# A hand-kept global order of 975 steps is replaced by a new one, with other transfer rates in its planner

## The chip, the cores and the metric

The kernel runs on one core of a Trainium2 chip. The core has five engines that run beside each other and meet at semaphores: TensorE (PE in the profile; PEld is its weight load), VectorE (DVE), ScalarE (ACT), GpSimd (POOL) and SyncE (SP). Here SP does nothing but issue DMAs; ACT issues a few too. The metric is device time in microseconds (us), the median of several runs; smaller is better.

## What is computed

Polynomial-sketch attention over 4 batches, 4 heads, 1088 positions and head dimension 32, followed by a feed-forward layer on the 4352 tokens (width 128, hidden width 2048) with a rational activation:

```python
def phi(x):                                   # 8 x 8 sketch features of each position
    a = einsum('rd,bhsd->bhsr', S1, x)
    b = einsum('rd,bhsd->bhsr', S2, x)
    return einsum('bhsi,bhsj->bhsij', a, b).reshape(..., 64)
q_p, k_p = phi(q), phi(k)
kv  = einsum('bhsf,bhsd->bhfd', k_p, v)
z   = sum(k_p, axis=2)
x   = einsum('bhsf,bhfd->bhsd', q_p, kv) / (einsum('bhsf,bhf->bhs', q_p, z) + 1e-6)
h   = x @ w_in                                # 4352 x 128 by 128 x 2048
P   = a[0] + a[1]*h + a[2]*h*h + a[3]*h*h*h
Q   = 1 + |b[0]|*|h| + |b[1]|*h*h
out = (P / (Q + 1e-6)) @ w_out                # 2048 x 128
```

Inputs and output are float32.

## The kernel before

The whole program is a list of 975 steps, each for one engine: a DMA issue, a group of matmuls, an ACT or DVE instruction. `step(...)` and `dma(...)` append to the list; nothing is issued while it is built. At the end `run` sorts the steps by a number from the table `PLACE` and issues them in that order. Each engine works through its own steps strictly in this order, so `PLACE` decides who queues behind whom, on SP's and ACT's DMA queues too. Waits between engines follow from the data and from the buffers: a step that takes a buffer of a kind with few slots (`Buf("kq")` has 3, `v_sb` 1, `h`, `att` and `out` in PSUM 2 each, `a_all`, `b_all`, `sk_sb` and `sk_d` 2 each, `t` 16) takes the slot that has been free the longest and waits until its last reader is done.

The numbers given to a step besides its function (rank, cost, `rate`, `slack`, `early`, `behind`) belong to the planner that once computed `PLACE`. In the program itself they issue nothing and wait for nothing; `behind` and `after` are only used to assert that one step's place precedes another's. `ON_ACT` lists the numbers of steps that could run on ACT or DVE and run on ACT. `FILLS` says ahead of which places how many products of zeros (line L321) are put on PE.

What the steps do, with the lines of the profile:

- *Loads.* S1 and S2 (`s_raw`), k of the first batch (on ACT's queue), a first piece of q (256 of its 1088 columns), v in two halves, the rest of q, `w_out` in two halves (into the buffer `ln`), `w_in` in two halves, k of the second batch, then v and q of the second batch, and so on. All other loads are on SP's queue (L268).
- *keys*, once a batch: DVE transposes k (L415, L417), PE makes sketches (L435), ACT copies one factor (L440, `b_sk`), DVE multiplies to features `k_p` (L443), PE accumulates features by v (L454), ACT copies the sum to `kvz` (L471).
- *queries*, in pieces of up to 384 positions: DVE transposes q (L496). The first 512 positions are done "direct": PE writes both sketches expanded (L518), ACT copies (L523, L526), DVE multiplies (L530, L533). All later pieces are "spread": PE makes the plain sketches (L546), ACT copies them (L551, `sk_sb`), two DMAs put them to DRAM (`sk_d`), three DMAs get them back repeated (`a_all`, `b_all`), DVE multiplies (L554). Then, for both: products with kvz (L586), guard, inverse and quotient on DVE (L595, L599, L602), a transpose on PE (L608), a copy to `xT` on ACT (L615).
- *w_out* is converted to bf16 in five scaled versions of two halves each: ten steps, on ACT (L391 scaled, L393 plain) or DVE (L395 scaled).
- *a* and *b* are spread to all partitions by a product with ones (L377) and two ACT copies (L380, L381).
- *units*, 29 of them, of up to 6 blocks of 512 tokens: hidden products (L688), ACT evacuates them to bf16 (L692), then the activation: DVE takes |h| (L703), w = |b0| + |b1| |h| on DVE (L708) or ACT (L710), a product (L713), ACT ln and exp (L716, L719), a product with r (L728), and, in three ways of dividing the work ("modes"), further products on DVE (L731, L734, L737, L746, L749), p = a2 + a3 h on DVE (L723) or ACT (L725), the addition of a1 on DVE (L741) or ACT (L743). PE gathers with w_out (L784), DVE turns the result (L796), SP stores it (L808).

Of the kernel before, what the change touches and what calls it, by code (L numbers as in the profile page):

```python
# [20 lines left out]
def kernel(  # L21
# [15 lines left out]
    B, H, S, D = q.shape  # L37
# [87 lines left out]
    def d_four(n, ptr):  # L125
# [14 lines left out]
    LOADS = 1.3  # L140
# [5 lines left out]
    GET_SLACK = 0.9  # L146
# [67 lines left out]
    )  # L214
    ON_ACT = (
        24, 26, 28, 29, 31, 32, 328, 351, 379, 454, 478, 502, 535, 612, 636, 669, 688, 693, 744, 878, 889,
        914, 932, 946, 951, 953, 960,
    )
    FILLS = {5: 15, 14: 4, 66: 5, 70: 1}
# [36 lines left out]
    def flat(x, b):  # L256
        return x[b].rearrange("h (g j) d -> (h g) (j d)", g=32)
# [605 lines left out]
```

## Time and profile before

| | |
|---|---|
| median of 3 runs | 266.75 us (266.74 to 267.11) |
| profiled execution | 267.34 us; its span, from first to last instruction, 265.5 us |
| busy: PE, DVE, ACT | 257.2, 252.7, 248.4 us |
| moved by DMA | 20.13 MB, mean 76 GB/s; 202 to 331 GB/s in the first 13 us |

A row of a timeline gives start in us from the start of the span, duration in us, engine, line, operation, output <- input, shapes, count (rows that stand close together are merged), and in square brackets how long the engine had been idle before and what the profile thinks ended that. SPq is SP's issuing of DMAs. A row of waits gives the engine and line that waited, what for, us in total, times, the longest. A row of groups gives the form, xcount, then busy us and mean ns of one, then idle us before. A row of the chain gives start, duration and what the chain was in.

### The profile page before, as it was taken

The numbers are of one execution on the slowest core, as the hardware profiler recorded it, in microseconds if no ns is written. First come the engines' busy times: TensorE is split into PE (matmuls) and PEld (weight loads), VectorE is DVE, ScalarE is ACT, GpSimd is POOL, SyncE is SP. The second block draws the span as 40 slices with busy tenths as digits, with TensorE's granted clock in tenths as the row PEclk, the third lists the DMA queues.
The fourth block names the chain that finished last, engine by engine and source line by source line (L and its number), as shares of the span: only waits on it lengthen the run. The fifth ranks groups of instructions, "written<-read, shape, count | busy, mean of one in ns | idle before, by whom it ended". The sixth has DMA issues, their size and how long they took to land.

```text
span 265.5 us, 4239 instructions
## 1 busy us (share of the span) xinstructions
PE 257.2 (97%) x1663; PEld 140.4 (53%) x1663; DVE 252.7 (95%) x293; ACT 248.4 (94%) x209; POOL 2.7 (1%) x25
## 2 busy tenths in 40 slices
PE   7999999999999999999999999999999999999994
PEld 5767645644544464344445555444444476565682
DVE  3989899999999999999999999999999999999994
ACT  2499999999999999999999999999999999999991
POOL 4000000000000000000000000000000000000000
PEclk9999999999999999999999999999999999999998
DMA  7948344620556503035001522200002002010032
GB/s 202 331 151 223 121 127 118 159 61 0 145 131 168 164 2 108 13 79 131 28 6 44 150 65 46 41 0 0 0 10 32 0 0 40 4 29 11 0 52 40
DMA packets 29063, 20.13 MB, mean 76 GB/s; under 512 B 19316, under 2 KB 24948, under 8 KB 29044
## 3 DMA queue, kind: packets, MB, share of 16 engines
q1 hardware_dynamic: 28352, 19.24, 28.8%
q10 hardware_dynamic: 692, 0.62, 0.8%
q8 instruction: 13, 0.21, 0.4%
q14 instruction: 6, 0.05, 0.1%
HBM read 16.65 MB, written 3.21 MB: 75 GB/s over the span
## 4 chain that ended last, share of the span: by engine, by line
PE 35%; ACT 29%; DVE 21%; issue 8%; DMA 4%; SPq 1%; DVEq 0%; ACTq 0%
PE h_ps L688 21%; ACT t L692 7%; ACT ln L716 7%; ACT t L719 7%; PE out_ps L784 6%; ACT t L725 5%; DVE t L713 4%; DVE t L728 4%; DVE t L731 3%; DMA kq<-in_q_dram 3%; DVE t L749 2%; PE att_ps L586 2%; DVE t L703 2%; PE att_ps L546 2%; DVE t L708 2%
## 5 line engine op out<-in xcount | busy, mean ns | idle before, releaser
L688 PE MATMUL h_ps<-xT,w_in_sb 128*128 128x512 f32 (+1 forms) x320 | 128.0, 535 | 0.8 <-ACT xT L615 0.6
L784 PE MATMUL out_ps<-t,w_out 128*128 128x512 bf16 (+1 forms) x498 | 101.7, 346 | 0.6 <-DVE t L728 0.5
L688 PEld LDWEIGHTS h_ps<-xT,w_in_sb 128*128 128x128 f32 x320 | 58.6, 190 | 45.2 <-issue 33.8
L784 PEld LDWEIGHTS <-w_out 128*128 128x128 bf16 x498 | 47.4, 98 | 51.9 <-issue 21.1
L692 ACT CAST t<-h_ps 128x1024 bf16<-128x1024 f32 (+1 forms) x69 | 68.5, 1025 | 0.9 <-PE h_ps L688 0.9
L716 ACT ACTIVATE ln<-t 128x3072 f32<-128x3072 bf16 (+4 forms) x29 | 64.7, 2230 | 0.3 <-DVE t L713 0.2
L719 ACT ACTIVATE t<-ln 128x3072 bf16<-128x3072 f32 (+4 forms) x29 | 64.7, 2232 | 0.1
L713 DVE TENSOR_TENSOR t<-t,t 128x3072 bf16<-128x3072 bf16 (+4 forms) x29 | 40.4, 1392 | 0.6 <-ACT t L710 0.6
L728 DVE TENSOR_TENSOR t<-t,t 128x3072 bf16<-128x3072 bf16 (+4 forms) x29 | 40.4, 1394 | 0.0
L731 DVE TENSOR_TENSOR t<-t,t 128x3072 bf16<-128x3072 bf16 (+3 forms) x23 | 32.6, 1423 | 0.1
L725 ACT ACTIVATE t<-t,a_sb 128x3072 bf16<-128x3072 bf16 (+2 forms) x12 | 32.0, 2665 | 0.0
L703 DVE TENSOR_SCALAR t<-t 128x3072 uint16<-128x3072 uint16 (+4 forms) x29 | 22.5, 776 | 0.3 <-ACT t L692 0.2
L734 DVE TENSOR_TENSOR t<-t,t 128x3072 bf16<-128x3072 bf16 (+1 forms) x13 | 21.6, 1660 | 0.0
L708 DVE TENSOR_SCALAR t<-t,b_abs 128x3072 bf16<-128x3072 bf16 (+2 forms) x22 | 21.5, 975 | 0.1
L586 PEld LDWEIGHTS att_ps<-kvz,a_all 128*64 128x64 f32 x288 | 9.6, 137 | 6.8 <-issue 2.2
L586 PE MATMUL att_ps<-kvz,a_all 128*64 128x66 f32 x288 | 11.5, 226 | 0.6 <-DVE a_all L530 0.4
L749 DVE TENSOR_TENSOR t<-t,t 128x1024 bf16<-128x1024 bf16 (+3 forms) x10 | 11.2, 1124 | 0.1
L710 ACT ACTIVATE t<-t,b_abs 128x1024 bf16<-128x1024 bf16 (+4 forms) x7 | 11.3, 1611 | 0.0
L554 DVE TENSOR_TENSOR a_all<-a_all,b_all 128x768 f32<-128x768 f32 (+2 forms) x11 | 9.6, 869 | 0.0
L443 DVE TENSOR_TENSOR k_p<-att_ps,b_sk 128x768 f32<-128x768 f32 x9 | 8.4, 949 | 0.8 <-ACT b_sk L440 0.6
L454 PEld LDWEIGHTS att_ps<-v_sb,k_p 128*64 128x64 f32 x216 | 6.7, 138 | 2.3 <-issue 1.3
L746 DVE TENSOR_TENSOR t<-t,t 128x3072 bf16<-128x3072 bf16 (+3 forms) x6 | 7.7, 1276 | 0.0
(74 smaller groups left out, 143.8 us busy)
## 6 DMA issues: line engine op xcount, KB each, us to landing
a_all<-sk_d SPq DMA_DIRECT2D x6, 384.0 KB, 3.9
b_all<-sk_d SPq DMA_DIRECT2D x12, 192.0 KB
kq<-in_k_dram SPq DMA_DIRECT2D x3, 544.0 KB, 7.3
kq<-in_q_dram SPq DMA_DIRECT2D x3, 544.0 KB
a_all<-sk_d SPq DMA_DIRECT2D x4, 320.0 KB
b_all<-sk_d SPq DMA_DIRECT2D x8, 160.0 KB
v_sb<-in_v_dram SPq DMA_DIRECT2D x4, 288.0 KB, 4.9
v_sb<-in_v_dram SPq DMA_DIRECT2D x4, 256.0 KB, 4.3
```

The lines of the kernel that those rows point to most:

```text
L586: nc.tensor.matmul(nd.t[x:x + 64, o:o + 2 * KW], lhsT=(av(c)[:, o0 + x:o0 + x + 64] if how == "direct" else q_p.t[:, c * n + o0 + x:c * n ...
L688: nc.tensor.matmul(h.t[:, cols[x] - cols[x0]:cols[x + 1] - cols[x0]], lhsT=w_in_sb[:, f * 128:(f + 1) * 128], rhs=xT[:, xpos(t0):xpos(t0) ...
L692: nc.scalar.copy(out=hh.t[:, cols[x0]:cols[x1]], in_=h.t[:, 0:cols[x1] - cols[x0]])
L703: nc.vector.tensor_scalar(out=u.t[:, :n].bitcast(U16), in0=hh.t[:, :n].bitcast(U16), scalar1=0x7FFF, scalar2=None, op0=AX.bitwise_and)
L708: nc.vector.tensor_scalar(out=w.t[:, :n], in0=u.t[:, :n], scalar1=ab1, scalar2=ab0, op0=AX.mult, op1=AX.add)
L713: nc.vector.tensor_mul(out=y.t[:, :n], in0=w.t[:, :n], in1=u.t[:, :n])
L716: nc.scalar.activation(out=ln.t[:, :n], in_=y.t[:, :n], func=ACT.Ln, bias=1.0 + 1e-6)
L719: nc.scalar.activation(out=r.t[:, :n], in_=ln.t[:, :n], func=ACT.Exp, scale=-1.0)
L725: nc.scalar.activation(out=p.t[:, :n], in_=hh.t[:, :n], func=ACT.Identity, scale=a3, bias=a2)
L728: nc.vector.tensor_mul(out=s.t[:, :n], in0=hh.t[:, :n], in1=r.t[:, :n])
L731: nc.vector.tensor_mul(out=(hh if mode == 3 else p).t[:, :n], in0=hh.t[:, :n], in1=s.t[:, :n])
L784: nc.tensor.matmul(o[0].t[:, :bl[x][1]], lhsT=w_sb[y_][:, bl[x][2], :], rhs=src.t[:, cols[x]:cols[x + 1]], start=(o[1] == 1), stop=(o[1] = ...
```

## The change

The planner's rates and slacks for the transfers are set to others and the order is computed anew. In the program this means: all of `PLACE` is replaced (shown cut below), `ON_ACT` and `FILLS` change in a few entries, and in the lists of what must precede what the second batch's v and q loads are put behind the last get of the first spread piece, and the product that spreads a and b behind the first sketch of keys. No step is added or removed, and no step's work is changed, but for the eight whose engine changes and four zero products fewer.

```diff
-    GET_SLACK = 0.9
+    GET_SLACK = 1.2
...
     PLACE = (
-        0, 3, 1, 19, 6, 7, 8, 2, 18, 16, 9, 58, 55, 12, 10, 4, 5, 13, 24, 25, 49, 21, 23, 22, 83, 97, 84,
-        71, 82, 59, 96, 68, 105, 61, 11, 28, 14, 20, 27, 37, 17, 30, 31, 41, 36, 38, 39, 43, 32, 33, 35, 44,
...
+        0, 3, 1, 8, 4, 5, 10, 2, 9, 18, 13, 71, 16, 17, 11, 6, 7, 14, 19, 21, 15, 29, 33, 30, 80, 46, 91,
+        66, 83, 58, 111, 43, 90, 101, 12, 24, 22, 23, 25, 38, 26, 27, 28, 39, 36, 40, 42, 48, 37, 41, 47,
...
     ON_ACT = (
-        24, 26, 28, 29, 31, 32, 328, 351, 379, 454, 478, 502, 535, 612, 636, 669, 688, 693, 744, 878, 889,
-        914, 932, 946, 951, 953, 960,
+        25, 26, 29, 31, 32, 33, 328, 342, 344, 379, 454, 478, 502, 535, 612, 636, 669, 688, 693, 744, 878,
+        889, 914, 932, 951, 953, 960,
     )
-    FILLS = {5: 15, 14: 4, 66: 5, 70: 1}
+    FILLS = {7: 15, 22: 4, 70: 1, 77: 1}
...
-    k0_l = load_k(0, k0, -207, slack=0.0, rate=304, eng=ACTE)
+    k0_l = load_k(0, k0, -207, slack=0.15, rate=420, eng=ACTE)
...
-    v0_l = load_v(0, v0, -203.7, slack=0.25, rates=(180, 200), behind=q0_a)
+    v0_l = load_v(0, v0, -203.7, slack=0.4, rates=(340, 205), behind=q0_a)
...
-    k1_l = load_k(1, k1, K1L_RANK, early=LATER, slack=0.2, behind=v0_l[1], rate=350)
+    k1_l = load_k(1, k1, K1L_RANK, early=LATER, slack=1.3, behind=v0_l[1], rate=390)
...
-    st = step(PE, 0.11, mk_ab, AB_RANK, after=ab_in, uses=[ab_ps])
+    st = ab_st = step(PE, 0.11, mk_ab, AB_RANK, after=ab_in, uses=[ab_ps])
...
+            if wide and x == 0:
+                ab_st.after.append(sk)
...
-                               rank, n * 0.512e-3, put, [d, bb], rate=85, cost=0.6, slack=GET_SLACK, behind=get[-1]))
-
+                               rank, n * 0.512e-3, put, [d, bb], rate=95, cost=0.6, slack=GET_SLACK, behind=get[-1]))
+
+            gets.append(get[-1])
...
-        vl = load_v(b, vb, LOADS - 0.01 if b == 1 else base - 13.9, gate, slack=1.5 if b == 1 else V_SLACK, behind=w_l[1] if b == 1 else None)
-        ql = dma(lambda qb=qb: qb.t, flat(q, b), LOADS if b == 1 else base - 13.8, 0.557, gate, [qb], rate=250, slack=1.5 if b == 1 else V_SLACK, behind=puts[1] if b == 1 else None)
+        vl = load_v(b, vb, LOADS - 0.01 if b == 1 else base - 13.9, gate, slack=1.5 if b == 1 else V_SLACK, behind=gets[0] if b == 1 else None)
+        ql = dma(lambda qb=qb: qb.t, flat(q, b), LOADS if b == 1 else base - 13.8, 0.557, gate, [qb], rate=250, slack=1.5 if b == 1 else V_SLACK, behind=gets[0] if b == 1 else None)
```

What becomes of the order at the start, queue by queue (first steps after v has been issued; "..." are steps that the change leaves where they are):

```
SP  before: rest of q | w_out, w_out | w_in, first half | k of batch 2 | put | w_in, second half | put |
            a_all, b_all, b_all | v, v of batch 2 | put, put of the next piece | q of batch 2 | a_all, ...
SP  after:  w_out | rest of q | k of batch 2 | w_out | w_in, first half | put, put | w_in, second half |
            put, put of the next piece | a_all, b_all, b_all | v, v of batch 2 | q of batch 2 | a_all, ...
ACT before: ... b_sk | kvz | sk_sb | w_out | L523 | w_out | xT | w_out x3 | L692 | xT | sk_sb | w_out | ...
ACT after:  ... w_out | b_sk | w_out | kvz | sk_sb | w_out | L523 | sk_sb | xT | w_out x2 | L692 | xT | w_out | xT | ...
PE  before: ... L546 | L518 | L586 | L518 | zeros | L608 | zeros | L586 | L688 | L608 | L546 | L688 | ...
PE  after:  ... L546 | L518 | L586 | L518 | L546 | zeros | L608 | zeros | L586 | L688 | L608 | L608 | L688 | ...
```

In the changed kernel lines from L435 on stand up to 3 lower down in the file.

More of the change, by code (lines that the diff above doesn't have):

```diff
@@ L292 @@
     FIRST = 256
-    k0_l = load_k(0, k0, -207, slack=0.0, rate=304, eng=ACTE)
+    k0_l = load_k(0, k0, -207, slack=0.15, rate=420, eng=ACTE)
     table = step(ACTE, 1.3, lambda: nc.scalar.preload_act_table_set("natural_log_exp_and_others"), -205, behind=k0_l[0])
-    q0_a = dma(lambda: q0.t[:, 0:FIRST], flat(q, 0)[:, 0:FIRST], -203.8, 0.131, (), [q0], rate=250, slack=0.1, behind=s_l[1])
-    v0_l = load_v(0, v0, -203.7, slack=0.25, rates=(180, 200), behind=q0_a)
+    q0_a = dma(lambda: q0.t[:, 0:FIRST], flat(q, 0)[:, 0:FIRST], -203.8, 0.131, (), [q0], rate=350, slack=0.2, behind=s_l[1])
+    v0_l = load_v(0, v0, -203.7, slack=0.4, rates=(340, 205), behind=q0_a)
     ab_in = []
@@ L304, in load_w @@
         c = x * 1024
-        w_l[x] = dma(w_in_sb[:, c:c + 1024], moe_w_in[:, c:c + 1024], rank, 0.524, early=LATER, rate=300, slack=0.4, behind=v0_l[1])
+        w_l[x] = dma(w_in_sb[:, c:c + 1024], moe_w_in[:, c:c + 1024], rank, 0.524, early=LATER, rate=430, slack=0.4, behind=v0_l[1])
     load_w(0, -196)
-    q0_b = dma(lambda: q0.t[:, FIRST:S], flat(q, 0)[:, FIRST:S], Q0B_RANK, 0.426, (), [q0], rate=200, slack=0.3, behind=q0_a)
+    q0_b = dma(lambda: q0.t[:, FIRST:S], flat(q, 0)[:, FIRST:S], Q0B_RANK, 0.426, (), [q0], rate=330, slack=0.4, behind=q0_a)
     load_w(1, W1_RANK)
     k1 = Buf("kq")
-    k1_l = load_k(1, k1, K1L_RANK, early=LATER, slack=0.2, behind=v0_l[1], rate=350)
+    k1_l = load_k(1, k1, K1L_RANK, early=LATER, slack=1.3, behind=v0_l[1], rate=390)
     wo_l = [dma(lambda f0=f0: w_raw.t.rearrange("p (f d) -> p f d", d=d_model)[:, f0:f0 + nf // 2],
                 moe_w_out.rearrange("(fo fi) d -> fi fo d", fi=128)[:, f0:f0 + nf // 2], WO_RANK, 0.525, (), [w_raw],
-                early=LATER, rate=310, slack=0.4, behind=v0_l[1]) for f0 in (0, nf // 2)]
+                early=LATER, rate=318, slack=0.4, behind=v0_l[1]) for f0 in (0, nf // 2)]
     idle = consts.tile([128, 256], BF, name="idle")
@@ L483, in turns @@
         return ((0, m),) if x >= m else ((0, x), (x, m))
-    puts = []
+    puts, gets = [], []
     def queries(b, qb, q_l, c0, c1, rank, how, pre=None, pre2=None, apart=False, early=0.0, size=1):
@@ L562, in queries @@
                        lambda j=j: c.t[j * 2 * half:(j + 1) * 2 * half, :n2],
-                       rank, n2 * 256e-6, [st], [c, d], rate=260, slack=GAP) for j in range(2)]
+                       rank, n2 * 256e-6, [st], [c, d], rate=200, slack=GAP) for j in range(2)]
             puts[-1] = put[-1]
@@ L566, in queries @@
                        lambda: bass.AP(tensor=d.t.tensor, offset=d.t.offset, ap=[[2 * QN, 2 * R], [0, R], [1, 2 * n]]),
-                       rank, n * 1.024e-3, put, [d, a], rate=230, cost=0.57, slack=GET_SLACK)]
+                       rank, n * 1.024e-3, put, [d, a], rate=230, cost=0.57, slack=GET_SLACK - 0.2)]
             for h2 in range(2):
```

92 rows, old and new, of the table PLACE are left out of this document.

## The prediction

> **What bounds the kernel now.** I read the page first, then the waits of the single engines, then the timeline of the first 32 us, where the edits act, and two later places where VectorE (DVE) stands still.
>
> ```profile
> span 265.5 us, 4239 instructions
> PE 257.2 (97%) x1663; PEld 140.4 (53%) x1663; DVE 252.7 (95%) x293; ACT 248.4 (94%) x209; POOL 2.7 (1%) x25
> PE 35%; ACT 29%; DVE 21%; issue 8%; DMA 4%; SPq 1%; DVEq 0%; ACTq 0%
> ```
>
> TensorE (PE), DVE and ScalarE (ACT) are each busy for 94 to 97% of the span, and the chain that ended last passes through all three. None of them hides work of another. A change of order that keeps the work can win only the idle 5%: of DVE's 265.5 - 252.7 = 12.8 us. DVE's own waits say where these lie.
>
> ```profile
> DVE s_rep L352 <- DMA s_raw<-in_S_dram: 4.5, 1, 4.5
> DVE qT L496 <- DMA kq<-in_q_dram: 0.7, 1, 0.7
> DVE t L713 <- ACT t L710: 0.6, 1, 0.6
> ...
> 250.00:265.50 15.50, 11.59 (x103) 9.86 (x101) 11.67 (x21) 9.89 (x12) 0.00 (x0) 0.93 0.27 39
> ```
>
> The first 4.5 us (the first load of S) and the last 15.50 - 11.67 = 3.8 us (the drain of the last unit and its stores) are not touched: the S loads stay at the head of their queue, and the last DVE and PE steps stand in nearly the same order. That leaves 12.8 - 4.5 - 3.8 = 4.5 us of DVE idle time that an order can remove, and nothing bounds what it can add. Columns of the windows row: stretch and length, then busy us of PE, weight load, DVE, ACT, POOL, then granted clock, DMA share, GB/s.
>
> **Part 1, the second batch's q load.** This is the one DMA wait on the chain after the start.
>
> ```profile
> 12.61 1.32 SPq L268 DMA_DIRECT2D w_in_sb<-in_moe_w_in_dram  x1
> 18.07 0.56 SPq L268 DMA_DIRECT2D a_all<-sk_d  x1
> 20.01 1.85 SPq L268 DMA_DIRECT2D v_sb<-in_v_dram  x2
> 21.91 1.25 SPq L268 DMA_DIRECT2D sk_d<-sk_sb  x2
> 23.20 7.33 DMA kq<-in_q_dram
> 30.55 0.58 DVE L496 STREAM_TRANSPOSE qT<-kq 128x384 f32<-128x384 f32 x1 [0.73 <-DMA kq<-in_q_dram]
> 31.27 0.55 PE L546 MATMUL att_ps<-qT,S 128*64 128x192 f32 x4 [0.56 <-DVE qT L496]
> ```
>
> In SP's queue q waits behind both puts of the second sketch (21.91), and these wait for an ACT copy that stands late. The new order puts that copy directly before the first xT copy on ACT, and both pairs of puts ahead of the first get. The gets need both first puts to have landed, and those no longer stand on either side of the second w_in half. SP then issues, from the first sketch's copy on (near 12.5, Part 2): two puts 1.25, w_in 1.32, two puts 1.25, and stands at the gets at 16.3 instead of 18.07, when the first puts, issued by 13.7, should be down. Gets and v take 23.20 - 18.07 - 1.25 = 3.9 us, so q is issued near 20.2, 3 us before 23.20, and with the same 7.33 us lands near 27.5. DVE could have begun this transpose at 30.55 - 0.73 = 29.8; the new order puts two element steps fewer ahead of it, so near 29. DVE's 0.73 and PE's 0.56 go. Below: nothing is gained if SP stands still at the gets; above: 0.73. I take 0.73. What comes next there is U3's evacuation on ACT, which the new order puts behind this transpose; it ends just ahead of the product that needs its PSUM buffer.
>
> **Part 2, the start of the first hidden product.** Before:
>
> ```profile
> 11.26 0.43 ACT L471 COPY kvz<-out_ps 64x66 f32<-64x66 f32 x2 [1.70 <-PE out_ps L454]
> 11.87 1.05 ACT L393 CAST w_out<-ln 128x1024 bf16<-128x1024 f32 x1
> 12.15 0.69 PE L586 MATMUL att_ps<-kvz,a_all 128*64 128x66 f32 x16
> 13.52 0.59 ACT L523 COPY a_all<-h_ps 128x512 f32<-128x512 f32 x1 [0.59 <-PE h_ps L518]
> 13.96 0.38 PE L608 MATMUL att_ps<-ident,x_tok 128*128 128x128 f32 x2
> 14.00 1.15 ACT L391 ACTIVATE w_out<-ln,a_sb 128x1024 bf16<-128x1024 f32 x1
> 14.13 0.69 DVE L530 TENSOR_TENSOR a_all<-h_ps,a_all 128x512 f32<-128x512 f32 x1 [0.39 <-ACT a_all L523]
> 14.88 1.04 PE L586 MATMUL att_ps<-kvz,a_all 128*64 128x66 f32 x16 [0.43 <-DVE a_all L530]
> 15.05 0.36 ACT L615 COPY xT<-att_ps 128x256 f32<-128x256 f32 x1
> 15.85 1.99 PE L688 MATMUL h_ps<-xT,w_in_sb 128*128 128x256 f32 x8
> 17.88 0.49 PE L546 MATMUL att_ps<-qT,S 128*64 128x160 f32 x4
> ```
>
> Now a w_out half is loaded right behind v, and two conversions of it (1.15 us each) stand on ACT ahead of the kvz copy, in the idle 1.70. The half's last byte is number 1.77 MB (k 0.56, the first piece of q 0.13, v 0.56, w_out 0.52).
>
> ```profile
> 0.00:5.00 5.00, 3.46 (x17) 2.34 (x18) 0.49 (x2) 1.28 (x1) 2.38 (x23) 1.00 0.62 194
> 5.00:10.00 5.00, 4.62 (x93) 3.75 (x93) 4.94 (x15) 1.62 (x9) 0.36 (x2) 1.00 1.11 280
> 10.00:13.00 3.00, 3.00 (x64) 2.33 (x62) 2.59 (x7) 1.63 (x4) 0.00 (x0) 1.00 1.14 356
> 13.00:14.00 1.00, 1.00 (x10) 0.61 (x9) 0.68 (x3) 0.48 (x2) 0.00 (x0) 1.00 0.94 364
> 14.00:15.00 1.00, 0.57 (x9) 0.29 (x8) 0.86 (x2) 1.00 (x2) 0.00 (x0) 1.00 0.49 86
> ```
>
> 194 GB/s for 5 us is 0.97 MB; the other 0.80 at 280 GB/s end at 7.9 us. Allow 1.5 us until all engines have reported it: 9.4. Then kvz is copied at 9.4 + 1.15 + 0.2 (the copy of b_sk between) + 1.15 = 11.9, which is 0.6 later than 11.26 (short copies are taken at 0.2, as the two that make up the 0.43). What repays it: no w_out conversion stands between ACT's L523 and the xT copy any more (14.00 in the rows above). Kvz 11.9 + 0.43, products 0.69, then the guard, inverse, quotient and turn back (from 12.15 + 0.69 to 13.96 + 0.38 before, 1.5 us) give 14.5, xT 14.9. ACT's own queue: kvz until 12.3, sketch copy 0.2, cast 1.05, L523 0.59, sketch copy 0.2: 14.4, no later. L530 runs from 14.2 to 14.9, the 1.04 of products to 15.8 less the wait in it: the hidden product starts at 15.6 to 15.9, 15.65 taken. It also needs w_in's first half, now behind the k load: its last byte is number 3.81 MB, and 0.97 + 1.40 + 1.07 + 0.36 = 3.80 MB have passed by 14.0, so it lands at 14 to 15.5. PE therefore gains 0.2 (0 to 0.25). The L546 at 17.88 moves ahead of this start, into PE's hole (0.57 busy in 14 to 15): another 0.42 that PE, full from 15.85 on, no longer pays, taken whole.
>
> DVE meets this at its first d_abs, which waits for the first evacuation. That comes 0.2 earlier, and one conversion of w_out fewer stands ahead of it, so I count DVE even.
>
> **Part 3, PE earlier by 0.2 + 0.4 + 0.56 = 1.2 us from 31 us on.** Two later waits of DVE come from PE being late.
>
> ```profile
> 47.44 0.92 PE L586 MATMUL att_ps<-kvz,a_all 128*64 128x66 f32 x24
> 48.48 0.17 DVE L595 TENSOR_SCALAR rec<-att_ps 128x12 f32<-128x12 f32 x1 [0.48 <-ACT t L692]
> 87.93 1.01 ACT L692 CAST t<-h_ps 128x1024 bf16<-128x1024 f32 x1 [0.42 <-PE h_ps L688]
> 88.83 2.95 ACT L725 ACTIVATE t<-t,a_sb 128x3072 bf16<-128x3072 bf16 x1
> 91.94 0.96 DVE L443 TENSOR_TENSOR k_p<-att_ps,b_sk 128x768 f32<-128x768 f32 x1 [0.62 <-ACT b_sk L440]
> ```
>
> At 48.48 the guard starts when the products end (47.44 + 0.92), whatever engine the row names. At 91.94 the b_sk copy stands behind the 2.95 us L725, which stands behind an evacuation that had waited 0.42 for PE. With PE 1.2 us ahead both lose their cause: 0.48 + 0.62 = 1.1, if the new order keeps as many steps between them; bounds 0 and 1.1, 1.1 taken. The other DVE wait (0.6 on L710, an ACT activation) I leave in.
>
> **Part 4, steps that change engine.** Of ten w_out conversions two go from DVE to ACT and two back, one of them the plain cast. A 1024-wide and a 768-wide w = |b0| + |b1|·u go from ACT to DVE; a 1024-wide p and a 1024-wide addition of a1 go from DVE to ACT.
>
> ```profile
> L395 DVE TENSOR_SCALAR w_out<-ln,a_sb 128x1024 bf16<-128x1024 f32 x4 | 2.9, 736 | 0.0
> L708 DVE TENSOR_SCALAR t<-t,b_abs 128x1024 bf16<-128x1024 bf16 x3 | 1.6, 543 | 0.1
> L723 DVE TENSOR_SCALAR t<-t,a_sb 128x1024 bf16<-128x1024 bf16 x1 | 0.5, 496 | 0.0
> L710 ACT ACTIVATE t<-t,b_abs 128x1024 bf16<-128x1024 bf16 x2 | 2.5, 1252 | 0.0
> L725 ACT ACTIVATE t<-t,a_sb 128x1024 bf16<-128x1024 bf16 x1 | 1.3, 1261 | 0.0
> ```
>
> DVE: + 0.54 + about 0.45 (somewhat over three quarters of 0.54) - 2 x 0.50, the conversions even (a cast on DVE has no row; not above 0.74): 0.0. ACT: - 1.25 - about 1.0 + 1.26 + about 1.25 + 0.1 (1.15 against the cast's 1.05): + 0.4. ACT is as full as the others, but ended its last activation before DVE; bounds 0 and + 0.4, and I put 0 in the sum because DVE closes the span. The planner's rates and slacks issue nothing themselves; they only produced PLACE. The matmul for a and b stands behind the same sketches as before: 0. The 22 instead of 26 zero products stand in holes of PE.
>
> **Sum.** The whole order after 30 us is new, so new waits must be expected. Bounds: 0, and the 4.5 us of today again. I put in 0.6, about half of the 1.4 that I left standing (0.6, and 0.8 in small ones). On DVE, which closes the span: - 0.73 - 1.1 + 0.0 + 0.6 = - 1.2. The profiled execution took 267.34 (span 265.5 and 1.84 around it); it would become 266.1. The median of the runs is 0.59 below the profiled one: 266.75 - 1.2 = 265.6.
>
> **Rivals.** *The order gives it back:* three full engines in step at one place need not be so at the next; the new waits reach 1.8 instead of 0.6. For it: the order has 975 steps, nearly all moved. Against: PE no longer falls behind at the start, the cause of most waits that the rows show. Time 266.2 to 267.3; chance 0.18. That q comes no earlier (SP held at the gets) belongs here: the 0.73 and 0.56 stay, and of the rest about 0.4: 266.35.
>
> *ACT blocks itself, slower:* the two conversions ahead of b_sk and kvz wait for their w_out half, and ACT serves in order; behind them stand the last b_sk copy, kvz, and with kvz every product of queries. Each us that the half lands after 9.4 delays the first hidden product by one. From 10.3 on the start is worse than 15.85. The old trace shows only that a half was there by 11.87; landing then would cost 2.5 us at the start, 1.8 after what q and the sketch still give: 268.5. Against it: the byte count says 7.9. Chance with its milder forms and a worse tail of the order above 0.19.
>
> *The clock falls:* fewer zero products, while PE has holes before 15.6. The rows show 1.00 granted in each stretch, with PE 57% busy in the emptiest. Were the first hidden product to run at half rate, its 1.99 us would cost 2 more: 267.6, chance 0.03. The Trainium skill, "TensorE: Matmul & The Clock Gate", Part 1, says that the array's clock is halved after an idle window of about 3.4 us and needs as long a busy one to come back. By that rule the holes here, under 1 us each, are too short; the trace agrees so far, 1.00 throughout the start.
>
> **Numbers.** Faster 0.60, within 0.2% 0.18, slower 0.22 (0.2% is 0.53 us, about what a measurement of this kernel can tell from no change). Range 264.7 to 267.7: below, no new waits and the 0.6 on L710 gone too (265.6 - 0.9); above, the first rival whole and the slower one half paid.
>
> **What would show it.** Right: the first hidden product at 15.6 to 15.9, q's transpose with no DMA wait, no DVE wait near 48 and 92, DVE idle outside start and end near 3.3 us. Wrong: ACT idle behind the kvz copy's turn before 12 us, a DVE wait on q, or new waits in DVE's list that sum to over 1.8 us between 30 and 250 us.

## The result and the profile after

The changed kernel takes 265.94 us in the median (265.84 to 266.03), where the kernel before took 266.83 beside it (266.74 to 267.23). The ratio is 0.9963, 95% interval 0.9951 to 0.9976: about 0.9 us faster. One of its seven executions, at 439.29 us with a granted clock of 0.56, is left out of the range and of the ratio. The profiled execution took 265.84 us, 0.1 below the median of its kernel; that of the kernel before (267.34) lay 0.5 above its own.

The head of the page of the changed kernel, and the first line of its chain:

```profile
span 264.1 us, 4201 instructions
PE 254.8 (96%) x1641; PEld 141.1 (53%) x1659; DVE 252.4 (96%) x293; ACT 248.5 (94%) x209; POOL 2.7 (1%) x25
ACT 51%; PE 30%; DVE 10%; issue 8%; POOL 0%; ACTq 0%; POOLq 0%
```

DVE's busy time is nearly the same (252.4 against 252.7), so 1.1 of the 1.4 us of span that went are idle time. The 4% of DMA in the chain of before are gone, and ACT has 51% of it, where it had 29%. Where the idle time went is read from windows with the same cuts in both traces (stretch, length, then busy us of PE, weight load, DVE, ACT, POOL, granted clock, DMA share, GB/s). The kernel before:

```profile
0.00:20.00 20.00, 17.52 (x212) 13.05 (x212) 14.06 (x39) 11.02 (x24) 2.74 (x25) 1.00 0.78 229
20.00:31.00 11.00, 10.72 (x157) 8.17 (x155) 9.89 (x19) 10.43 (x15) 0.00 (x0) 1.00 0.69 202
31.00:100.00 69.00, 68.59 (x420) 34.04 (x420) 67.89 (x79) 67.50 (x60) 0.00 (x0) 1.00 0.39 104
100.00:180.00 80.00, 79.33 (x477) 37.80 (x477) 79.18 (x78) 79.66 (x56) 0.00 (x0) 1.00 0.25 59
```

The changed kernel, with its last stretch:

```profile
0.00:20.00 20.00, 17.81 (x208) 13.06 (x209) 13.43 (x38) 11.50 (x24) 2.75 (x25) 1.00 0.81 243
20.00:31.00 11.00, 10.97 (x155) 8.24 (x154) 10.95 (x22) 11.00 (x17) 0.00 (x0) 1.00 0.71 180
31.00:100.00 69.00, 68.02 (x447) 35.10 (x450) 68.33 (x81) 68.17 (x60) 0.00 (x0) 1.00 0.40 110
100.00:180.00 80.00, 78.66 (x467) 38.37 (x474) 79.45 (x76) 79.96 (x55) 0.00 (x0) 1.00 0.24 54
...
250.00:264.10 14.10, 9.90 (x88) 8.31 (x86) 10.29 (x20) 7.89 (x11) 0.00 (x0) 1.00 0.30 44
```

Length less DVE's busy time gives its idle time, before and after:

| stretch | before | after | difference |
|---|---|---|---|
| 0 to 20 us | 5.94 | 6.57 | + 0.63 |
| 20 to 31 | 1.11 | 0.05 | - 1.06 |
| 31 to 100 | 1.11 | 0.67 | - 0.44 |
| 100 to 180 | 0.82 | 0.55 | - 0.27 |
| from 250 on | 3.83 | 3.81 | 0.0 |

From 180 to 250 us DVE is never idle in either. So the change loses at the start and wins behind it. The timeline of the changed kernel shows what it lost, and DVE's waits name it:

```profile
7.46 0.65 ACT L528 COPY a_all<-att_ps 128x256 f32<-128x256 f32 x2 [0.45 <-PE att_ps L520]
7.89 0.97 PE L520 MATMUL att_ps<-qT,SAB 64*128 64x256 f32 x4 [0.46 <-ACT a_all L528]
9.63 1.15 ACT L391 ACTIVATE w_out<-ln,a_sb 128x1024 bf16<-128x1024 f32 x1
11.92 0.43 ACT L473 COPY kvz<-out_ps 64x66 f32<-64x66 f32 x2
13.48 0.59 ACT L525 COPY a_all<-h_ps 128x512 f32<-128x512 f32 x1
14.12 0.70 PE L520 MATMUL h_ps<-qT,SAB 64*128 64x256 f32 x4 [0.62 <-ACT a_all L525]
14.95 0.69 DVE L532 TENSOR_TENSOR a_all<-h_ps,a_all 128x512 f32<-128x512 f32 x1 [0.54 <-PE h_ps L520]
15.72 0.37 ACT L618 COPY xT<-att_ps 128x256 f32<-128x256 f32 x1
16.53 1.99 PE L691 MATMUL h_ps<-xT,w_in_sb 128*128 128x256 f32 x8
20.30 0.60 SPq L268 DMA_DIRECT2D kq<-in_q_dram  x1
29.11 0.96 DVE L498 STREAM_TRANSPOSE qT<-kq 128x384 f32<-128x384 f32 x2
```

```profile
DVE a_all L535 <- PE att_ps L520: 0.5, 1, 0.5
DVE a_all L532 <- PE h_ps L520: 0.5, 1, 0.5
...
DVE t L726 <- ACT ln L719: 0.4, 1, 0.4
```

A "direct" sketch consists of two products that fill the two halves of one PSUM buffer (L520), an ACT copy of the first half (L528, L525) and DVE's product with the second half (L535, L532). The old order ran both products and then the copy. The new order puts the copy between them. The second product then waits until ACT has read the buffer: 0.46 us at 7.89 and 0.62 at 14.12. The first hidden product starts at 16.53 instead of 15.85.

### The profile page after: what moved, and what is told of

The parts are those of the page before. It is cut to its first block, busy times and chain, and to the rows that moved or that the text cites. A ratio compares the mean times of both kernels' runs of the same rounds, so it can differ in the third digit from the quotient of the medians.

```text
span 264.1 us, 4201 instructions
## 1 busy us (share of the span) xinstructions
PE 254.8 (96%) x1641; PEld 141.1 (53%) x1659; DVE 252.4 (96%) x293; ACT 248.5 (94%) x209; POOL 2.7 (1%) x25
## 4 chain that ended last, share of the span: by engine, by line
ACT 51%; PE 30%; DVE 10%; issue 8%; POOL 0%; ACTq 0%; POOLq 0%
PE h_ps L691 14%; ACT ln L719 13%; ACT t L722 13%; ACT t L695 11%; PE out_ps L787 7%; ACT t L728 6%; ACT t L713 3%; DVE t L734 2%; DVE t L737 2%; PE att_ps L589 1%; DVE t L731 1%; PE att_ps L548 1%; DVE t L716 1%; PE att_ps L321 1%; PE att_ps L435 1%
## 5 line engine op out<-in xcount | busy, mean ns | idle before, releaser
L787 PE MATMUL out_ps<-t,w_out 128*128 128x512 bf16 (+1 forms) x480 | 97.8, 344 | 1.9 <-issue 1.1
L695 ACT CAST t<-h_ps 128x1024 bf16<-128x1024 f32 (+1 forms) x69 | 69.4, 1053 | 0.5 <-PE h_ps L691 0.4
L719 ACT ACTIVATE ln<-t 128x3072 f32<-128x3072 bf16 (+4 forms) x29 | 65.5, 2257 | 0.3 <-DVE t L716 0.2
L722 ACT ACTIVATE t<-ln 128x3072 bf16<-128x3072 f32 (+4 forms) x29 | 65.4, 2254 | 0.2
L728 ACT ACTIVATE t<-t,a_sb 128x3072 bf16<-128x3072 bf16 (+2 forms) x13 | 33.3, 2574 | 0.4 <-PE out_ps L787 0.4
L711 DVE TENSOR_SCALAR t<-t,b_abs 128x3072 bf16<-128x3072 bf16 (+3 forms) x24 | 22.3, 928 | 0.0
L713 ACT ACTIVATE t<-t,b_abs 128x2048 bf16<-128x2048 bf16 (+3 forms) x5 | 9.0, 1809 | 0.1
```

The costliest lines, as they stand in the source:

```text
L695: nc.scalar.copy(out=hh.t[:, cols[x0]:cols[x1]], in_=h.t[:, 0:cols[x1] - cols[x0]])
L719: nc.scalar.activation(out=ln.t[:, :n], in_=y.t[:, :n], func=ACT.Ln, bias=1.0 + 1e-6)
L722: nc.scalar.activation(out=r.t[:, :n], in_=ln.t[:, :n], func=ACT.Exp, scale=-1.0)
L728: nc.scalar.activation(out=p.t[:, :n], in_=hh.t[:, :n], func=ACT.Identity, scale=a3, bias=a2)
L787: nc.tensor.matmul(o[0].t[:, :bl[x][1]], lhsT=w_sb[y_][:, bl[x][2], :], rhs=src.t[:, cols[x]:cols[x + 1]], start=(o[1] == 1), stop=(o[1] = ...
```

## Experiments on the start

**The copy behind both products.** In the changed kernel, the second products of both sketches go ahead of the copies:

```diff
+    PLACE = list(PLACE)
+    PLACE[60] = 34.5
+    PLACE[22] = 34.6
+    PLACE[71] = 63.5
```

> The changed kernel with three numbers of the order altered: the two ACT copies of the first direct query pieces come after the second sketch product that fills the other half of the same PSUM buffer, as before the change, not ahead of it. Nothing else moves on any engine. Theory A (the copy placed ahead makes PE wait until ACT has read the buffer, 0.46 us at 7.89 and 0.62 at 14.12, and this set the late start at 16.53): both PE waits go, the first hidden product starts at 15.6 to 15.9, DVE's 0.55 at 8.62 and 0.54 at 14.95 go too, and the time falls by 0.5 to 0.9 us below the changed kernel, to 265.0 to 265.4. Rival B (the start was late for another reason, the kvz copy behind two conversions of w_out): the waits go but the hidden product stays at 16.2 or later, the time within 0.3 of 265.9. Rival C (the later order absorbs an earlier start): hidden product earlier, time the same.

Measured: 265.61 us, 0.9962 of the kernel before (0.9942 to 0.9982; 266.92 on that chip); profiled 265.16, span 263.4. PE's waits on the two copies are gone, and the first hidden product comes 0.6 us earlier than in the changed kernel:

```profile
15.92 1.99 PE L695 MATMUL h_ps<-xT,w_in_sb 128*128 128x256 f32 x8
```

**Both pairs of products side by side**, the second pair also ahead of the attention products of the first piece, and beside it **the changed kernel again**, on one chip:

```diff
+    PLACE = list(PLACE)
+    PLACE[60] = 34.5
+    PLACE[22] = 34.6
+    PLACE[70] = 60.5
+    PLACE[71] = 61
```

> The changed kernel with both products of each query sketch side by side on TensorE, ahead of the ScalarE copy of the first half, for both query pieces. Theory (ScalarE's reading of one half of the buffer makes TensorE wait before it writes the other): the waits of 0.46 and 0.62 on these copies go, the first hidden product is at 15.9 or earlier instead of 16.53, and the time is 265.2 (264.9 to 265.5). Rival (the start is not what the end follows): the first product is earlier and the time stays within 0.2 of the changed kernel's.

> The changed kernel as it is, beside the other three, to have their differences on one chip. Both theories: 265.9 (265.8 to 266.1), and 0.996 of the kernel before.

Measured: 265.52 us, 0.9942 (0.9929 to 0.9955), against 265.95 us, 0.9973 (0.9952 to 0.9995), for the changed kernel. The waits on the copies are gone here too. The first hidden product came only at 16.33, because a load was now the last to arrive, which I had not expected:

```profile
16.33 0.92 PE L696 MATMUL h_ps<-xT,w_in_sb 128*128 128x256 f32 x3 [0.28 <-DMA w_in_sb<-in_moe_w_in_dram]
```

By medians the two mended kernels are 0.3 to 0.4 us faster than the changed one, and they are the fastest versions of this study. The intervals do not settle it: the first has the ratio of the changed kernel (0.9962 and 0.9963, on different chips), and those of the second and its neighbour on one chip overlap slightly. The sign rests on the medians of two kernels and on the waits that vanish. In the profiled executions the gain at the first hidden product arrives whole: 0.61 earlier and 0.68 shorter for the first (265.16 against 265.84), 0.51 and 0.52 for the second (265.59 against 266.11 for the changed kernel on the same chip, whose product started at 16.84).

**The mirror.** In the kernel before, the copies go between the products:

```diff
+    PLACE = list(PLACE)
+    PLACE[60] = 28.5
+    PLACE[71] = 61.5
```

> The kernel before with one edit, the mirror of the run in which the sketches stood together: for both query pieces the ScalarE copy of the first half of the sketch is put between the two products on TensorE, as the new order has it. Theory (a read of one half of the buffer makes the write of the other wait): TensorE waits about 0.4 to 0.6 us ahead of each second product, the first hidden product comes at 16.3 to 16.6 instead of 15.85, and the time rises by 0.4 to 0.7, to 267.3 (267.1 to 267.6) where the kernel before takes 266.9. Rival (the start has slack, the waits on the query load further on take the loss up): the waits are there and the time stays within 0.2.

Measured: 267.99 us, 1.0035 of the kernel before (1.0024 to 1.0046), which is + 0.6 to + 1.2 us. The waits appear where they were put:

```profile
PE h_ps L521 <- ACT a_all L526: 0.8, 1, 0.8
...
PE att_ps L521 <- ACT a_all L529: 0.4, 1, 0.4
```

The profiled execution of this kernel took 270.7 us, with a granted clock of 0.50 from 8 to 12 us; its rows show that the waits are there, not what they cost in an ordinary run. The direction is the theory's; by medians the loss is 1.1, more than the 0.4 to 0.7 it gave, and what makes up the rest is open.

**The w_out half late.** In the changed kernel the two loads of `w_out` change places, so that the half needed first comes behind other loads and ACT, which has its conversions ahead of the kvz copy, has to wait for it. This is the rival "ACT blocks itself", made to happen:

```diff
+    PLACE = list(PLACE)
+    PLACE[14] = 17
+    PLACE[13] = 11
```

> The changed kernel with the two w_out loads exchanged: the half that two ACT conversions ahead of the kvz copy need is the later one, behind q and k. It prices the rival of the prediction, ACT blocking itself. Theory A (ACT serves in order and everything of the queries stands behind kvz): the half lands near 12 instead of 9.5, the first conversion starts there, kvz is copied near 14.4 instead of 11.92, the first hidden product starts 2.0 to 2.5 us later than 16.53, and the time rises by 1.5 to 2.5 us to 267.4 to 268.4. Rival B (a later start is absorbed, since DVE and ACT have idle time at the start anyway): hidden product 2 us later, time up by less than 1 us.

Measured: 271.24 us, 1.016 (1.0138 to 1.0182). The long waits of ACT and PE, and two windows:

```profile
13.35 1.15 ACT L394 ACTIVATE w_out<-ln,a_sb 128x1024 bf16<-128x1024 f32 x1 [3.83 <-DMA ln<-in_moe_w_out_dram]
15.09 0.69 PE L457 MATMUL out_ps<-v_sb,k_p 128*64 128x64 f32 x8 [3.74 <-DVE k_p L446]
21.95 1.99 PE L694 MATMUL h_ps<-xT,w_in_sb 128*128 128x256 f32 x8
```

```profile
14.00:18.00 4.00, 2.91 (x28) 1.94 (x30) 2.25 (x5) 3.71 (x8) 0.00 (x0) 0.56 0.04 8
18.00:22.00 4.00, 4.00 (x39) 2.31 (x35) 2.31 (x6) 1.20 (x4) 0.00 (x0) 0.58 0.47 147
```

ACT starts the conversion at 13.35 instead of 9.63, 3.7 later. The first hidden product comes 5.4 later, 1.7 more than that, because PE had stood idle for 3.74 us and was then granted a lower clock: the two windows have 0.56 and 0.58 in the mean, and cut into windows of one us the record shows 0.50 in each from 15 to 21. Its product L523 of four takes 1.23 us there, where 0.70 is usual (L520 in the changed kernel, 14.12 above). The kernel's time rises by 5.3 us, far more than the 1.5 to 2.5 expected, since the half came 3.7 later rather than 2.5 and the clock had not been reckoned with. What the first hidden product loses, the end loses; no wait further on takes it up.

**No products of zeros** in the changed kernel:

```diff
-    FILLS = {7: 15, 22: 4, 70: 1, 77: 1}
+    FILLS = {}
```

> The changed kernel without any of its 21 idle products on zeros. Theory (they only hold the clock): with TensorE busy on real work from 5 us on the granted clock stays at 0.99 or more, and the time is within 0.3 of the changed kernel's 265.9. Rival (without the first 15 products the clock is low in the first microseconds): the granted clock falls to 0.7 or less in a slice of the first 13 us, the first hidden product comes 0.3 us or more later, and the time is 266.3 to 267.

Measured: 268.59 us, 1.0056 (1.0032 to 1.008), some 2.6 us slower than the changed kernel. Both expectations missed: the loss is larger than either gave, and the granted clock shows 1.00 in every window of the first 24 us. Yet the real products of the start are much slower. PE's groups from 5 to 13 us (form, count, busy us, mean ns), without the zeros:

```profile
L520 PE MATMUL att_ps<-qT,SAB 64*128 64x256 f32 x8 | 2.7, 711 | 0.5 <-ACT a_all L528 0.5
L435 PE MATMUL h_ps<-S,kT 128*64 128x64 f32 x26 | 2.1, 318 | 1.0 <-DVE S L355 1.0
```

and with them, in the changed kernel:

```profile
L520 PE MATMUL att_ps<-qT,SAB 64*128 64x256 f32 x8 | 1.7, 428 | 0.5 <-ACT a_all L528 0.5
L435 PE MATMUL h_ps<-S,kT 128*64 128x64 f32 x28 | 1.4, 225 | 0.0
```

The rival named the right place, the first microseconds, but the granted clock that was to show it did not. The first hidden product comes 2.65 us later than in the changed kernel, as much as the time grows:

```profile
19.18 1.99 PE L691 MATMUL h_ps<-xT,w_in_sb 128*128 128x256 f32 x8
```

**What the start is worth.** Six profiled executions so far share the order behind the start. Their first hidden products begin at 15.92 to 21.95 us, and the time from there to the end is the same in all of them within 0.15 us (profiled time less that start):

| kernel | first hidden product | profiled time | difference |
|---|---|---|---|
| changed kernel | 16.53 | 265.84 | 249.31 |
| changed kernel again | 16.84 | 266.11 | 249.27 |
| copy behind both products | 15.92 | 265.16 | 249.24 |
| both pairs side by side | 16.33 | 265.59 | 249.26 |
| no products of zeros | 19.18 | 268.52 | 249.34 |
| w_out half late | 21.95 | 271.34 | 249.39 |

In the new order a delay of the first hidden product thus costs its full length. The kernel before has 15.85 and 267.34, so 251.49 from there on. By these profiles the change loses 0.68 us up to the first hidden product and wins 2.18 behind it.

## Experiments on the q load and the later waits

**The q load late**, in the changed kernel behind the next three gets:

```diff
+    PLACE = list(PLACE)
+    PLACE[117] = 105.5
```

> The changed kernel with one number altered: the q load of the second batch is issued behind the three gets of the second spread piece instead of ahead of them. Theory A (the earlier q load is worth its wait, 0.73 on DVE): q is issued near 22.5 instead of 20.3, lands near 29.5 to 30, DVE waits 0.3 to 0.9 us at its transpose (29.1), PE about as long, and the time rises by 0.3 to 0.9 us to 266.2 to 266.8. Rival B (q was hidden either way, since its transfer is faster with less behind it): no wait, 265.9 within 0.2.

Measured: 269.27 us, scattered from 266.6 to 274.3, 1.0051 (1.0011 to 1.009). The load was issued at 22.68, and the wait came back with twice the size it had in the kernel before:

```profile
31.09 0.97 DVE L500 STREAM_TRANSPOSE qT<-kq 128x384 f32<-128x384 f32 x2 [1.51 <-DMA kq<-in_q_dram]
```

The profiled execution, 267.87 us, is 2.0 us above that of the changed kernel, and its later waits are the same, only shifted. Its first hidden product starts at 16.91, 0.38 later; the other 1.65 lie behind it, about as long as the wait (1.51 on DVE). So the new order needs q early. The price is larger than the 0.3 to 0.9 of Theory A, whose wait was to be 0.3 to 0.9 as well. The other executions scatter: in seven of the twelve the mean granted clock was 0.987 to 0.994, and the five at 0.998 to 1.00 took 266.61 to 268.11 and once 271.13. Why the clock fell is open; only one execution was profiled.

**The q load early, alone**, in the kernel before: ahead of the v loads, nothing else moved.

```diff
-    ... behind=puts[1] if b == 1 else None)
+    ... behind=None)
+    PLACE = list(PLACE)
+    PLACE[117] = 87.5
```

> The kernel before with one number altered: its q load of the second batch is issued ahead of the v loads and the two puts, near 20.0 instead of 23.2. Theory A (that wait is a good part of what the new order wins): DVE's wait of 0.73 at 30.55 goes, later waits shrink with PE 0.5 us earlier, the time falls by 0.5 to 1.0 us to 265.8 to 266.3. Rival B (v then lands late: the products of features by v wait instead, 27.3 in the trace of before): a PE wait of 0.5 to 1.5 on v, the time 266.5 to 267.3. Rival C (the old order gives the gain back later): wait gone, time within 0.2 of 266.8.

Measured: 267.99 us, 1.0035 (1.002 to 1.005): slower, not faster, and beyond the range of Rival B too. The wait for q is gone; one for v has come, and the two waits further on are as before (PE, then DVE):

```profile
27.84 1.62 PE L456 MATMUL att_ps<-v_sb,k_p 128*64 128x64 f32 x48 [0.44 <-DMA v_sb<-in_v_dram]
48.36 0.17 DVE L597 TENSOR_SCALAR rec<-att_ps 128x12 f32<-128x12 f32 x1 [0.47 <-ACT t L694]
91.83 1.82 DVE L445 TENSOR_TENSOR k_p<-att_ps,b_sk 128x768 f32<-128x768 f32 x2 [0.62 <-ACT b_sk L442]
```

An early q load has to fit between the loads that are due before it. Here it was pushed ahead of v, which was due first. What this costs an ordinary execution the trace does not show: the profiled one, 267.27, is the fastest of the twelve and as fast as that of the kernel before (267.34).

**Mixtures of the two orders.** The first has the first 93 steps of the old order, then the new one; the second the first 96 of the new, then the old; the third the first 136 of the old (to about 28 us), then the new. In all three, `FILLS` and the engines of the w_out conversions go with the start, and q of the second batch follows the v loads directly.

> The changed kernel in which the first 93 steps of the order (up to about 17 us) stand as in the kernel before, with its halves of w_out and its idle products; all later steps stand in the new order, and the second batch's q load comes straight behind its v loads. Theory (the start and the rest are worth their idle time one by one: the new start costs 0.8 us, the new rest gives 1.7): the first hidden product at 15.8, no DVE waits near 48 and 92, 265.1 (264.8 to 265.5), 0.8 below the changed kernel. Rival (the places only work together, a better start is given back by waits further on): 265.8 or more, and a DVE wait of 0.3 us or more beyond 40 us that the changed kernel does not have.

> The other way round: the kernel before in which the first 96 steps stand as in the new order (halves of w_out and idle products too), all later ones as before; the second batch's q load comes with that start, early. Theory: the start's 0.8 us is added, the q wait of 0.73 goes but comes back in small waits behind it as when the q load alone was moved, and the DVE waits of 0.5 and 0.6 near 48 and 92 stay: 267.6 (267.2 to 268.0). Rival (the gain is in the start and its loads): 266.3 or less.

> The changed kernel in which the first 136 steps (up to about 28 us) stand as in the kernel before, so that the two orders meet where they differ by only four steps; the second batch's q load follows its v loads directly. In the first such mixture, cut at 93 steps, ScalarE stood in line behind a back transpose at 20 us and VectorE lost 0.9 us twice. Theory (that was the seam; start and rest add up by their own idle time): first hidden product at 15.8 to 16.3, no VectorE wait over 0.5 between 17 and 30 us, the later waits those of the changed kernel (0.2, 0.2, 0.2, 0.4), 265.3 (264.9 to 265.7). Rival (the new rest needs the state that the new start leaves): new waits of 0.5 us or more after 28 us and 266.2 or more.

Measured: 267.16 us, 1.0001 (0.9974 to 1.0028), for the first; 266.89, 0.999 (0.9971 to 1.001), for the second; 266.66, 0.9977 (0.9938 to 1.0015), for the third. None differs measurably from the kernel before. DVE's longest waits behind the start, in the first, the second and the third mixture:

```profile
20.15 0.43 DVE L706 TENSOR_SCALAR t<-t 128x1024 uint16<-128x1024 uint16 x1 [0.87 <-ACT t L695]
...
23.34 0.43 DVE L706 TENSOR_SCALAR t<-t 128x1024 uint16<-128x1024 uint16 x1 [0.93 <-ACT t L695]
```

```profile
48.06 0.17 DVE L595 TENSOR_SCALAR rec<-att_ps 128x12 f32<-128x12 f32 x1 [0.48 <-ACT t L692]
...
91.52 1.82 DVE L443 TENSOR_TENSOR k_p<-att_ps,b_sk 128x768 f32<-128x768 f32 x2 [0.62 <-ACT b_sk L440]
```

```profile
29.63 0.69 DVE L740 TENSOR_TENSOR t<-t,t 128x1024 bf16<-128x1024 bf16 x1 [0.88 <-ACT t L728]
```

In the second mixture the DMA wait for q is gone, and PE has no idle time left between 20 and 31 us. The waits at 48 and 92 us stay at 0.48 and 0.62 all the same. At 48 us both PE and DVE run 0.42 us ahead of the kernel before, so this does not tell what a lead of PE over DVE would do; it shows that coming earlier together leaves the waits of the old order as they are. The loss of the new start and the gain from q cancel in the median, where 267.6 was expected. This mixture also prices the rest of the order: it shares its first 96 steps with the changed kernel, which took 265.95 on the same chip, so the order behind these steps is worth 0.94 us. The profiles agree: from the first hidden product on it takes 250.30 us (266.89 less 16.59), between the 251.49 of before and the 249.31 of the changed kernel.

The first and third lose their gain where the orders meet. In the first, the evacuation L695 ahead of 20.15 stands behind three conversions of w_out in a row, and the one ahead of 23.34 behind an xT copy that stood ahead of its turn and made ACT wait 0.82 us. In the third, two activations of L728 follow each other. The theory of independent pieces could not be confirmed by them. A start and a rest that each look good do not join without a seam.

**The two waits taken out by hand**, in the kernel before, in the way the new order has it: at 48 us the products ahead of the hidden product, at 92 us the b_sk copy ahead of the long activation. The places in the changed kernel:

```profile
44.78 0.92 PE L589 MATMUL att_ps<-kvz,a_all 128*64 128x66 f32 x24
...
46.02 0.16 DVE L598 TENSOR_SCALAR rec<-att_ps 128x12 f32<-128x12 f32 x1
...
86.47 0.24 ACT L440 COPY b_sk<-att_ps 128x96 f32<-128x96 f32 x1
...
88.07 2.95 ACT L728 ACTIVATE t<-t,a_sb 128x3072 bf16<-128x3072 bf16 x1 [0.44 <-PE out_ps L787]
```

```diff
+    PLACE = list(PLACE)
+    PLACE[141] = 207.5
+    PLACE[142] = 216.5
+    PLACE[143] = 221.5
+    PLACE[144] = 222.5
+    PLACE[145] = 222.7
+    PLACE[188] = 362.5
+    PLACE[189] = 374.5
```

> The kernel before with seven of its steps moved at two places, nothing else. Near 48 us the sum of a_all and b_all (VectorE) goes ahead of the 1.7 us element step, the products on it ahead of the next hidden product on TensorE, and guard, inverse and quotient (VectorE) by up to nine places forward. Near 92 us a sketch product of k goes ahead of five gather groups on TensorE, and its b_sk copy ahead of the 2.95 us activation on ScalarE. Theory (the two waits are set by what stands next to them, not by TensorE being late from the start on): the DVE waits of 0.48 and 0.62 fall to 0.2 or less each, and the time falls by 0.7 to 1.1, to 266.0 (265.7 to 266.3) where the kernel before takes 266.9. Rival (three full engines: what is won there is lost at the next step): the two waits go, others of the same sum take their place within 10 us, and the time stays within 0.3.

Measured: 267.68 us, 1.0015 (0.9993 to 1.0037): no gain. Both waits are gone, and within 11 us of the second there are two others with nearly the same sum, 0.99 for 1.10:

```profile
46.96 0.16 DVE L603 TENSOR_SCALAR rec<-att_ps 128x12 f32<-128x12 f32 x1
...
95.17 1.76 DVE L736 TENSOR_TENSOR t<-t,t 128x3072 bf16<-128x3072 bf16 x1 [0.39 <-ACT t L727]
...
102.19 0.17 DVE L603 TENSOR_SCALAR rec<-att_ps 128x12 f32<-128x12 f32 x1 [0.60 <-PE att_ps L594]
```

The rival was right about the waits: what was won at one place was given back by the next steps, which had not been ordered anew. By medians the kernel is 0.5 us slower than the kernel before (267.17 on that chip), a little outside the 0.3 that the rival gave. One thing in this trace bears on the q load. The load is where the old order has it, but no wait shows:

```profile
23.55 0.59 SPq L276 DMA_DIRECT2D kq<-in_q_dram  x1
30.33 0.57 DVE L504 STREAM_TRANSPOSE qT<-kq 128x384 f32<-128x384 f32 x1
```

It had landed within 6.8 us of its issue. (The start of this execution was late: its first sixteen key products took 1.03 us where they took 0.69 before, at a granted clock of 1.00, and its first hidden product came at 16.44. So DVE came to the transpose 0.5 us later than the 29.8 of before; with 7.33 us the load would still have made it wait.) In the profiled execution of the kernel before it took 7.33, and in the kernel with q late about 8.4. The 0.73 us are thus not in every execution, which may be why that profile lay above its median. The runs without a profile cannot show it.

## Why the prediction was right, and where its steps failed

**Bounds.** Right: most of the gain came out of the idle 4.5 us. The tail kept its 3.8, and the first wait, on S, was 4.3 instead of 4.5. That leaves 264.1 - 252.4 - 4.3 - 3.8 = 3.6 us outside start and end, where 3.3 was forecast.

**Part 1, q load.** Right in what the trace shows: issued at 20.30 (20.2), transposed at 29.11 (near 29), no DMA wait. When the load landed (27.5 was forecast) no row says. The stretch from 20 to 31 us lost 1.06 us of DVE idle time, more than the 0.73. But the 0.73 was taken from one execution, and the moved load alone gave nothing in the old order. In the new order the wait is worth its length: with q late, 1.65 us went for a wait of 1.51.

**Part 2, the start.** This step failed. The w_out half (ACT came to it at 9.63 without a wait; in the two mended kernels ACT did wait for it, until 9.30 and 9.41; predicted 9.4, of which the 1.5 allowed for reporting has no row of its own), the kvz copy (11.92, predicted 11.9) and the first L525 copy (13.48) were close. The first hidden product came at 16.53, not at 15.6 to 15.9. The failed sentence is "ACT's own queue ... 14.4, no later. L530 runs from 14.2 to 14.9". I added up ACT's queue and DVE's, and let PE's second sketch product run whenever its data was there. The new order puts the ACT copy ahead of that product in the same buffer; PE stands still, and DVE's L532 starts at 14.95. "I count DVE even" was wrong by 0.63 us, although its wait on S was 0.2 shorter. The kernels with the products together and the mirror show this cause. In price, the mended kernels got back 0.3 to 0.4 by medians and 0.5 to 0.7 in the profiles, and the mirror lost 0.6 to 1.2. A second term stood on the edge: the first half of w_in, given for 14 to 15.5, was what PE waited for until 16.33 in the kernel with the pairs side by side.

**Part 3, the waits near 48 and 92 us.** Both went, but not for the reason given. PE being earlier is not enough: in the new start with the old rest, where PE was 0.42 us earlier at 48 us and DVE as well, both waits kept their size. Nor is it needed: the seven steps moved by hand took both out of the old order. What changed is the order around them. The 1.1 was right for the two rows and too high as a net on DVE: its idle time fell by 0.44 from 31 to 100 us, where 0.2 us waits came elsewhere, and by 0.71 up to 180 us (1.22 instead of 1.93). Taking the two out by hand won nothing. What won there was a whole order with fewer waits; against the second mixture it is worth 0.94.

**Part 4, engines.** DVE 252.7 to 252.4 and ACT 248.4 to 248.5 agree with 0.0 and the low end of 0 to + 0.4. The swaps were not run by themselves.

**Sum.** The terms were - 0.73 - 1.1 + 0.0 + 0.6 = - 1.2; DVE's idle time changed by - 1.06 - 0.44 - 0.27 + 0.63 = - 1.14. The 0.6 of new waits was a guess and had the right size, in a place where none was expected. The two errors, the lost start and the waits priced too high, were covered by that guess and by Part 1's larger share. That they cancel is luck: counted from the first hidden product the profiles win 2.18 behind it and lose 0.68 ahead of it, where the prediction had a gain of 0.2 at that point. "DVE closes the span" is also less than it seems, for the chain of the changed kernel runs mostly through ACT (51%); ACT's idle time fell by 1.5, from 17.1 to 15.6, and no term of the sum was on ACT's waits. The median fell by 0.9 rather than 1.2; the sum was made on a profiled execution that lay 0.5 above the median of its kernel, which may be why.

**Rivals.** "ACT blocks itself" did not come about, since the half landed in time, and its price was right as far as it went: one us at the first hidden product for each us of delay. Made to happen, it cost 3.7 us by that rule and 1.7 more, which goes with PE's lower clock after so long a hole. "The clock falls" did not come about either, 1.00 in every window; but the zero products were worth far more than I thought. "The order gives it back" is what the two waits taken out by hand showed. The q load moved alone and the three mixtures won nothing either, each for a cause of its own; the changed kernel gave back only its start.

## What to carry to other kernels

In this kernel with three nearly full engines, a later start of the first hidden product reached the end in full, in six profiles within 0.15 us. A wait further on is not by itself a price: taking two waits of 1.1 us out by hand won no time, and moving one load alone made it worse. When an order is read for its start, follow every reader and writer of each shared PSUM buffer, not only the data: in this program a copy placed between two products into one buffer stopped TensorE for 0.46 and 0.62 us. Sum such terms on more than one profiled execution, for the landing of a single load moved by over 0.5 us between two executions with the same order of loads.

## What the runs showed of the hardware

- Without products of zeros ahead, the first products ran at 711 instead of 428 ns (64x256) and 318 instead of 225 ns (128x64), up to about 13 us, with a granted clock of 1.00 in the record. The first hidden product came 2.65 us later and the kernel took 2.6 us longer than with the 21 zero products. The record of the granted clock does not show this slowness; the mean duration of one form does. The Trainium skill, "TensorE: Matmul & The Clock Gate", Part 1, says that the array starts at half rate and is released by a busy window of about 3.4 us. The trace agrees in kind; here, from the first real group at 5.62 us to about 13 us with one hole of 0.46 us, the slow phase lasted over twice as long.
- A hole of 3.74 us of TensorE was followed by a granted clock of 0.50 from 15 to 21 us (0.75 and 0.84 in the us before and behind). The Trainium skill, "TensorE: Matmul & The Clock Gate", Part 1, gives an idle window of about 3.4 us for this; the trace agrees. The first hidden product came 1.7 us later than ACT's delay of 3.7 alone explains.
- The same 544 KB load took from under 6.8 to about 8.4 us from issue to landing, in different executions and among different neighbours.
